# Attention and two feed-forward stages in one kernel: groups of five, four and three slices, two-deep staging

## The chip, the cores and the metric

The kernel runs on one core of a Trainium2 chip. The time is device microseconds of one execution on that core, the median of several runs.

## What is computed

```python
# q, k, v: (2, 8, 768, 64); block 32, window 16
scores_l = where(|i - j| < window, scale * q @ k^T, -1e9)      # local keys
scores_s = scale * q @ (max of k over each block)^T + log(32)  # 24 block keys
a = softmax(concat(scores_l, scores_s))
x = a @ concat(v, mean of v over each block)   # as 1536 tokens x 512
y = ((x @ w_a) * (x @ w_b)) @ w_out            # moe,  inner width 1536
out = leaky(y @ w_in) @ w_out2                 # moe2, inner width 2048, slope 0.01
```

The weights lie in memory as 64-bit floats.

## The kernel before

**Tiles.** The 1536 tokens are three chunks of 512 (`T`, `NC`). A chunk's attention output is four tiles `x` of 128 features, each kept as a high and a low part. The first stage's inner width is 12 slices of 128 (`NF1`), the second's 16. Every product of 32-bit accuracy is three matmuls (high by high, high by low, low by high; `mm3`, L583), so one slice of `x @ w_a` for one chunk is 12 matmuls of 128x512, and the same again for `w_b`.

**Weights.** A piece is one slice of one matrix, 512 KB. `stage` (L300) loads it into a tile `wst` (queue SP, L307 or L310); `convert` turns the 64-bit words into a high and a low part with six steps on DVE (VectorE: L332, L340, L345, L351, L357, L365) and two on ACT (ScalarE: L336, L362). The steps of a piece are spread among the other work of the two engines. `wst` has three buffers, and `convert` asks for up to four pieces ahead. L351 is the last step that reads `wst`. A piece is dropped when its last chunk has used it; 14 homes (`W_EARLY`) hold the converted pieces, 8 more (`W_LATE`) come once attention is over.

**First stage.** The 12 slices go in three groups of `M1` = 4, and for each group all three chunks are done in turn (`units`: group, chunk). Of a unit, each slice gives a product for `w_a` (bank `ps_a`, copied to `g` on ACT, L611), one for `w_b` (bank `ps_b`; DVE multiplies, L615), a high and a low part `gs` (L603 on ACT, L604 on DVE). Then `y_products` multiplies the unit's `gs` by the group's slices of `w_out`, and `gather` (L683, L685, L688) adds the sums of the groups.

**Attention among it.** Chunk 0's attention runs first, with the first two slices of group 0 beside it (`early`, banks a, b, c0, c1). Chunk 1's attention is woven into unit (0, 0), chunk 2's into unit (0, 1): its operations, cut at each large product, wait in `micro`, and `interleave` takes so many of them at each of four points of a slice that they last as long as the unit's remaining slices:

```python
todo = range(len(gs), M1)
...
pace["micro"] = len(micro) / (4 * len(todo) - 1.0)
```

Unit (0, 0) has two slices left to do (`todo`), since two were done beside chunk 0. What attention has per pair of score tiles: scores (L518 on PE, the TensorE; L531 on DVE; L535, the exponential, on ACT), normalizing (L543, L544, L545 on DVE), transposes of the probabilities (L553 on PE), values (L565 on PE, then L576 on DVE writes half of an x tile or a whole). Per half of the heads of a batch, `v` is loaded as `vb` (L154) and its blocks are summed by a set of three adds on POOL (GpSimd, L425) and two reductions on DVE (L435); there are four such sets. Key maxima are DVE's L482, their banks are filled by PE's L472.

**Order.** Each engine runs its instructions in a fixed order, found when the kernel is built: a scheduler with its own costs (L828) takes the operations by priority and by when their inputs and buffers are free. So a change of a number shifts rows on every engine. `q` tiles (L142) have three buffers, the tile `wr` of a conversion two.

Of the kernel before, what the change touches and what calls it, by code (L numbers as in the profile page):

```python
# [12 lines left out]
F32R = mybir.dt.float32r  # L13
I32 = mybir.dt.int32
# [7 lines left out]
def kernel(  # L22
# [14 lines left out]
    P = 128  # L37
# [17 lines left out]
    NF1 = F1 // P  # L55
    NF2 = F2 // P
    T = 512
    NT = B * S
    NC = NT // T
# [3 lines left out]
    assert GT == 2 * P and NB <= KP and KL + KP == P and D == 64 and KT == NP == NE  # L63


    M1 = 4
    M2 = 8
    W_EARLY, W_LATE = 14, 8

    const = ctx.enter_context(tc.tile_pool(name="const", bufs=1))  # L70
    xp = ctx.enter_context(tc.tile_pool(name="xp", bufs=NC * KT))
    wst_p = ctx.enter_context(tc.tile_pool(name="wst", bufs=3))
    wcv_p = ctx.enter_context(tc.tile_pool(name="wcv", bufs=2))
    wsp_p = ctx.enter_context(tc.tile_pool(name="wsp", bufs=W_EARLY))
    acc_p = ctx.enter_context(tc.tile_pool(name="acc", bufs=NE))
    g_p = ctx.enter_context(tc.tile_pool(name="g", bufs=2))
    psum = ctx.enter_context(tc.tile_pool(name="psum", bufs=1, space=bass.MemoryType.PSUM))
    att = ctx.enter_context(ExitStack())
    keep = att.enter_context(tc.tile_pool(name="keep", bufs=1))
    q_p = att.enter_context(tc.tile_pool(name="q", bufs=3))  # L80
    sm_p = att.enter_context(tc.tile_pool(name="sm", bufs=4))
    at_p = att.enter_context(tc.tile_pool(name="at", bufs=2))

# [37 lines left out]
    for j in range(2):  # L121
        t = xp.tile([P, BLK // 2, D], F32, tag="x", name=f"vb{j}")
# [129 lines left out]
    for kind in ("first", "mid", "last"):  # L252
        t = const.tile([P, P], F32, tag=f"negm_{kind}", name=f"negm_{kind}")
# [21 lines left out]

    units = [(s, c) for s in range(NF1 // M1) for c in range(NC)]
    slices2 = [(s * M2 + i, c) for s in range(NF2 // M2) for c in range(NC) for i in range(M2)]
    uses = []  # L280
    for s, c in units:
        fs = range(s * M1, (s + 1) * M1)
        uses += [(nm, f) for f in fs for nm in "ab"] + [("o", f) for f in fs]
    behind = []
    for f, c in slices2:
        uses += [("i", f), *behind]
# [29 lines left out]
    def convert():  # L316

        i = cnt["conv"]
        key = pieces[i]
        while cnt["st"] < min(i + 4, len(pieces)):  # L320
            stage()
        cnt["conv"] += 1
        ww = staged.pop(key).rearrange("p (f two) -> p f two", two=2)
        lo_w, hi_w = ww[:, :, 0], ww[:, :, 1]
        home = "early" if room["early"] else "late"
        assert room[home], key
        room[home] -= 1
        t = {}

        def low():  # L330
            t["r"] = wcv_p.tile([P, 512], I32, tag="wr", name="wr")
            nc.vector.tensor_scalar(  # L332
                out=t["r"], in0=lo_w.bitcast(U32), scalar1=2.0**-29, scalar2=None, op0=ALU.mult
            )
            t["c"] = wcv_p.tile([P, 512], I32, tag="wc", name="wc")
            nc.scalar.activation(out=t["c"].bitcast(F32), in_=hi_w.bitcast(F32), func=AF.Abs)  # L336

        def clamp():
            c = t["c"].bitcast(F32)
            nc.vector.tensor_scalar(  # L340
                out=c, in0=c, scalar1=F_LO, scalar2=F_HI, op0=ALU.max, op1=ALU.min
            )

        def shift():
            nc.vector.tensor_scalar(  # L345
                out=t["c"], in0=t["c"], scalar1=3, scalar2=0x3FFFFFF8,
                op0=ALU.logical_shift_left, op1=ALU.bitwise_and,
            )

        def join():  # L350
            nc.vector.scalar_tensor_tensor(  # L351
                out=t["c"], in0=hi_w, scalar=-0x40000000, in1=t["c"],
                op0=ALU.bitwise_and, op1=ALU.bitwise_or,
            )

        def add():
            nc.vector.tensor_tensor(out=t["c"], in0=t["c"], in1=t["r"], op=ALU.add)  # L357

        def high():
            pool = wsp_p if home == "early" else late["wsp"]  # L360
            t["w"] = pool.tile([P, 2, 512], F32R, tag="wsp", name="wsp")
            nc.scalar.copy(out=t["w"][:, 0], in_=t["c"].bitcast(F32))  # L362

        def rest_of():
            nc.vector.tensor_tensor(  # L365
                out=t["w"][:, 1], in0=t["c"].bitcast(F32), in1=t["w"][:, 0].bitcast(F32),
                op=ALU.subtract,
            )
            w_of[key] = t["w"], home

        bg.extend([low, clamp, shift, join, add, high, rest_of])
# [10 lines left out]
    def step():  # L382
        if bg:
            with tc.issue_after(pace["after"].ins) if pace["after"] is not None else nullcontext():
                bg.pop(0)()
# [3 lines left out]
    def weights(key):  # L389
        i = use_no["at"]  # L390
        assert uses[i] == key, (uses[i], key)
        use_no["at"] += 1
        while key not in w_of:
            if not bg:
                convert()
            step()
        w, home = w_of[key]
        if last_use[key] == i:
            spent.append(home)
            if key[0] != "o":  # L400
                free()
        return w
# [9 lines left out]
    xt = {}  # L412
# [186 lines left out]
        tick(int(cnt["bg"]))  # L599

    def parts(src):
        t = g_p.tile([P, 2, T], F32R, tag="gs", name="gs", bufs=M1)
        nc.scalar.copy(out=t[:, 0], in_=src)  # L603
        nc.vector.tensor_tensor(  # L604
            out=t[:, 1], in0=src, in1=t[:, 0].bitcast(F32), op=ALU.subtract
        )
        return t
# [38 lines left out]
    gs = [b_out(ab0["b", f][1], a_out(ab0["a", f][1])) for f in range(2)]  # L646
# [17 lines left out]
    def first_product(key, src, c):  # L664

        w = weights(key)
        ps = product_bank(key[0])
        for kt in range(KT):
            kt_mm(ps, w, src[c, kt], kt)
            if kt == KT // 2 - 1:  # L670
                interleave()
        return ps
# [3 lines left out]
    def gather(stage, c, e, ps, s, n):  # L676

        if s == 0:
            t = acc_p.tile([P, T], F32, tag="acc", name="acc") if (stage, c) not in late else (
                late[stage, c].tile([P, T], F32, tag="acc", name="acc"))  # L680
            sums[stage, c, e] = t
            if e % 2:
                nc.vector.tensor_copy(out=t, in_=ps)  # L683
            else:
                nc.scalar.copy(out=t, in_=ps)  # L685
            return t
        t = sums[stage, c, e]
        nc.vector.tensor_tensor(out=t, in0=ps, in1=t, op=ALU.add)  # L688
        return t
# [10 lines left out]

    def y_products(s, c, gs):

        ws = [weights(("o", s * M1 + i)) for i in range(M1)]

        def add(ps, e, i):
            mm3(
                ps,
                lambda j: ws[i][:, j, e * P : (e + 1) * P],
                lambda j: gs[i][:, j],
                i == 0, i == M1 - 1,  # L710
            )

        for e in range(0, NE, 2):
            ps = [product_bank("y") for _ in range(2)]

            for i0, i1 in ((0, M1 - 1), (M1 - 1, M1)):
                for j in range(2):
                    for i in range(i0, i1):
                        add(ps[j], e + j, i)
                    if i1 == M1:  # L720
                        if e + j == NE - 1:
                            free()
                        y = gather("y", c, e + j, ps[j], s, NF1 // M1)
                        if s == NF1 // M1 - 1:
                            y_parts(c, e + j, y)
                    interleave()

# [2 lines left out]
            micro.pop(0)[1]()  # L730

    for s, c in units:
        todo = range(len(gs), M1)
        pace["bg"] = {(0, 0): 4, (0, 1): 1, (0, 2): 3}.get((s, c), 1.3)
        if s == 0 and c + 1 < NC:

            last = PER * (sum(len(p) for p in pairs[: c + 2]) - 1) + PV
            micro += [o for o in later_ops if o[0] <= last]
            later_ops = later_ops[len(micro) :]
            pace["micro"] = len(micro) / (4 * len(todo) - 1.0)  # L740
            cnt["credit"] = 0.0
        for i in todo:
            pa = first_product(("a", s * M1 + i), xt, c)
            g = a_out(pa)
            interleave()
            pb = first_product(("b", s * M1 + i), xt, c)
            gs.append(b_out(pb, g))
            interleave()
        drain()
        if (s, c) == (0, NC - 2):  # L750

            att.close()
            late["wsp"] = ctx.enter_context(tc.tile_pool(name="wsp2", bufs=W_LATE))
            acc2 = ctx.enter_context(tc.tile_pool(name="acc2", bufs=2 * NE))
            late.update({(stage, c): acc2 for stage in "yo" for c in range(1, NC)})
            room["late"] = W_LATE
            turn.update({"a": ["a", "t0"], "b": ["b", "t1"], "y": ["c0", "c1", "t2", "t3"]})
            turn["i"] = ["a", "b", "t0", "t1"]
        y_products(s, c, gs)
        gs = []  # L760
# [25 lines left out]
    for f, c in slices2:  # L786
        ps = first_product(("i", f), ysp, c)
# [45 lines left out]
```

## Time and profile before

| | |
|---|---|
| median of 3 runs | 660.8 us (660.76 to 661.89) |
| the profiled execution | 661.53 us, its span 659.8 us |
| PE busy | 96% of the span, 3440 instructions |
| DVE busy | 63%, 952 instructions |
| ACT, POOL busy | 41%, 7% |
| chain that ended last | PE 88%, DVE 6%, POOL 2% |

The span lies between the first and the last instruction; 1.73 us of the profiled execution lie around it. An engine is busy while it has an instruction in work. The chain is followed back from the last instruction to what released each step.

### The profile page before, as it was taken

The numbers are of one execution on the slowest core, as the hardware profiler recorded it, in microseconds if no ns is written. First come the engines' busy times: TensorE is split into PE (matmuls) and PEld (weight loads), VectorE is DVE, ScalarE is ACT, GpSimd is POOL, SyncE is SP. The second block draws the span as 40 slices with busy tenths as digits, with TensorE's granted clock in tenths as the row PEclk, the third lists the DMA queues.
The fourth block names the chain that finished last, engine by engine and source line by source line (L and its number), as shares of the span: only waits on it lengthen the run. The fifth ranks groups of instructions, "written<-read, shape, count | busy, mean of one in ns | idle before, by whom it ended". The sixth has DMA issues, their size and how long they took to land.

```text
span 659.8 us, 9339 instructions
## 1 busy us (share of the span) xinstructions
PE 636.2 (96%) x3440; PEld 519.3 (79%) x3440; DVE 418.1 (63%) x952; ACT 270.8 (41%) x609; POOL 48.5 (7%) x79
## 2 busy tenths in 40 slices
PE   5797989999999999999999999999999999999997
PEld 4576767777888888888888888888888888888886
DVE  3999889955999962699623869732279532422323
ACT  3776787653545421344222535322255322222221
POOL 7254042000000000000000000000000000000000
PEclk9898999999999999999999999999999999999999
DMA  8997744512334430244200232400013000100101
GB/s 196 232 224 194 171 106 108 149 25 65 128 129 138 149 96 1 64 129 127 65 0 1 67 93 73 152 1 0 1 56 105 1 0 1 64 1 1 64 1 64
DMA packets 72622, 53.43 MB, mean 81 GB/s; under 512 B 46208, under 2 KB 66688, under 8 KB 72576
## 3 DMA queue, kind: packets, MB, share of 16 engines
q1 hardware_dynamic: 72576, 52.84, 28.0%
q8 instruction: 27, 0.44, 0.3%
q14 instruction: 19, 0.16, 0.1%
HBM read 49.68 MB, written 3.15 MB: 80 GB/s over the span
## 4 chain that ended last, share of the span: by engine, by line
PE 88%; DVE 6%; POOL 2%; DMA 1%; issue 1%; SPq 1%; ACT 0%; POOLq 0%; DVEq 0%
PE ps_t L583 38%; PE ps_c L583 18%; PE ps_a L583 14%; PE ps_b L583 13%; PE ps_t L518 2%; PE ps_t L565 1%; DVE pm L545 1%; PE ps_t L553 1%; DMA vb<-in_v_dram 1%; DVE pm L531 1%; POOL vb L425 1%; PE ps_t L472 1%; SPq L182 1%; DVE sm L543 0%; DVE acc L688 0%
## 5 line engine op out<-in xcount | busy, mean ns | idle before, releaser
L583 PE MATMUL ps_t<-x,wsp 128*128 128x512 f32 x336 | 78.4, 389 | 0.0
L583 PE MATMUL ps_c<-wsp,gs 128*128 128x512 f32 x288 | 75.9, 389 | 0.0
L583 PE MATMUL ps_t<-wsp,gs 128*128 128x512 f32 x288 | 74.7, 389 | 0.0
L583 PEld LDWEIGHTS ps_t<-x,wsp 128*128 128x128 f32 x336 | 63.1, 188 | 13.1
L583 PE MATMUL ps_t<-ys,wsp 128*128 128x512 f32 x288 | 71.9, 389 | 0.0
L583 PE MATMUL ps_a<-x,wsp 128*128 128x512 f32 x252 | 66.0, 399 | 1.8 <-ACT x L575 1.0
L583 PE MATMUL ps_b<-x,wsp 128*128 128x512 f32 x252 | 65.3, 395 | 0.0
L583 PEld LDWEIGHTS ps_t<-wsp,gs 128*128 128x128 f32 x288 | 54.0, 188 | 11.3
L583 PEld LDWEIGHTS ps_c<-wsp,gs 128*128 128x128 f32 x288 | 54.1, 188 | 11.2
L583 PEld LDWEIGHTS ps_t<-ys,wsp 128*128 128x128 f32 x288 | 54.1, 188 | 11.2
L583 PE MATMUL ps_c<-gs,wsp 128*128 128x512 f32 x240 | 61.0, 394 | 0.0
L336 ACT ACTIVATE wc<-wst 128x512 f32<-128x512 f32 x68 | 45.7, 674 | 28.9 <-DVE wsp L365 28.8
L362 ACT CAST wsp<-wc 128x512 fp32r<-128x512 f32 x68 | 42.1, 622 | 34.4 <-DVE wc L357 27.5
L583 PEld LDWEIGHTS ps_a<-x,wsp 128*128 128x128 f32 x252 | 46.8, 190 | 11.9 <-ACT x L575 1.3
L790 DVE SCALAR_TENSOR_TENSOR h<-h,ps_t 128x512 f32<-128x512 f32 x24 | 16.5, 686 | 60.3 <-ACT h L789 60.3
L583 PEld LDWEIGHTS ps_b<-x,wsp 128*128 128x128 f32 x252 | 46.6, 189 | 9.5 <-issue 0.3
L365 DVE TENSOR_TENSOR wsp<-wc,wsp 128x512 fp32r<-128x512 f32 x68 | 46.9, 693 | 8.5 <-ACT wsp L362 8.5
L583 PEld LDWEIGHTS ps_c<-gs,wsp 128*128 128x128 f32 x240 | 44.4, 188 | 9.6 <-DVE wr L332 0.2
L357 DVE CUSTOM_DVE_ANT_0 wc<-wc,wr 128x1024 uint16<-128x1024 uint16 x68 | 48.8, 718 | 0.5
L604 DVE TENSOR_TENSOR gs<-h,gs 128x512 fp32r<-128x512 f32 x48 | 33.1, 690 | 22.8 <-ACT gs L603 22.7
L583 PE MATMUL ps_t<-gs,wsp 128*128 128x512 f32 x192 | 47.5, 389 | 0.0
L351 DVE SCALAR_TENSOR_TENSOR wc<-wst,wc 128x512 int32<-128x512 int32 x68 | 46.6, 688 | 0.3
(94 smaller groups left out, 863.5 us busy)
## 6 DMA issues: line engine op xcount, KB each, us to landing
wst<-in_moe_w_out_dram SPq DMA_DIRECT2D x28, 512.0 KB, 3.3
wst<-in_moe_w_in_dram SPq DMA_DIRECT2D x16, 512.0 KB, 3.7
wst<-in_moe_w_a_dram SPq DMA_DIRECT2D x12, 512.0 KB, 4.4
wst<-in_moe_w_b_dram SPq DMA_DIRECT2D x12, 512.0 KB, 3.7
k<-in_k_dram SPq DMA_DIRECT2D x16, 192.0 KB, 3.6
vb<-in_v_dram SPq DMA_DIRECT2D x8, 384.0 KB, 5.4
out_dram<-acc SPq DMA_DIRECT2D x12, 256.0 KB, 2.0
q<-in_q_dram SPq DMA_DIRECT2D x16, 128.0 KB, 2.9
```

The costliest lines, as they stand in the source:

```text
L182: nc.sync.dma_start(out=t[p0 : p0 + o1 - o0, c, w0:w1, :], in_=src)
L336: nc.scalar.activation(out=t["c"].bitcast(F32), in_=hi_w.bitcast(F32), func=AF.Abs)
L351: nc.vector.scalar_tensor_tensor(out=t["c"], in0=hi_w, scalar=-0x40000000, in1=t["c"], op0=ALU.bitwise_and, op1=ALU.bitwise_or,)
L357: nc.vector.tensor_tensor(out=t["c"], in0=t["c"], in1=t["r"], op=ALU.add)
L362: nc.scalar.copy(out=t["w"][:, 0], in_=t["c"].bitcast(F32))
L365: nc.vector.tensor_tensor(out=t["w"][:, 1], in0=t["c"].bitcast(F32), in1=t["w"][:, 0].bitcast(F32), op=ALU.subtract,)
L425: nc.gpsimd.tensor_tensor(out=a, in0=a, in1=b, op=ALU.add)
L472: nc.tensor.transpose(ps[:, i * P : (i + 1) * P], k2[:, g * (GT // P) + i].rearrange("p c d -> p (c d)"), ident)
L518: nc.tensor.matmul(out=ps[h, w, :], lhsT=qt[h, w * W : (w + 1) * W], rhs=kts[h, (g * G + w) * SC : (g * G + w) * SC + P], start=True, stop ...
L583: nc.tensor.matmul(out=ps, lhsT=w(a), rhs=x(b), start=first and j == 0, stop=last and j == 2)
L604: nc.vector.tensor_tensor(out=t[:, 1], in0=src, in1=t[:, 0].bitcast(F32), op=ALU.subtract)
L790: nc.vector.scalar_tensor_tensor(out=h, in0=h, scalar=0.01, in1=ps, op0=ALU.mult, op1=ALU.max)
```

## The change

The first stage's slices go in groups of five, four and three (`group1`), and whatever depended on four slices takes the group's own range. One more home for converted weights (15) and one more `gs` buffer (5) hold the wider group. Staged weights `wst` and queries `q` are two deep instead of three, and `wr` is one deep. The products, conversions, loads and gathers are the same in number: only `todo` of unit (0, 0) has now three slices, that of unit (0, 1) five. In the changed kernel line numbers are higher by 1 to 3 (L583 is L585, L576 is L578, L351 is L353).

```diff
-    M1 = 4
+
+    M1 = (5, 4, 3)
     M2 = 8
-    W_EARLY, W_LATE = 14, 8
+    W_EARLY, W_LATE = 15, 8
...
-    wst_p = ctx.enter_context(tc.tile_pool(name="wst", bufs=3))
+    wst_p = ctx.enter_context(tc.tile_pool(name="wst", bufs=2))
...
-    q_p = att.enter_context(tc.tile_pool(name="q", bufs=3))
+    q_p = att.enter_context(tc.tile_pool(name="q", bufs=2))
...
-    units = [(s, c) for s in range(NF1 // M1) for c in range(NC)]
+    assert sum(M1) == NF1
+    group1 = [range(sum(M1[:s]), sum(M1[: s + 1])) for s in range(len(M1))]
+    units = [(s, c) for s in range(len(M1)) for c in range(NC)]
...
-        fs = range(s * M1, (s + 1) * M1)
-        uses += [(nm, f) for f in fs for nm in "ab"] + [("o", f) for f in fs]
+        uses += [(nm, f) for f in group1[s] for nm in "ab"] + [("o", f) for f in group1[s]]
...
-            t["r"] = wcv_p.tile([P, 512], I32, tag="wr", name="wr")
+            t["r"] = wcv_p.tile([P, 512], I32, tag="wr", name="wr", bufs=1)
...
-        t = g_p.tile([P, 2, T], F32R, tag="gs", name="gs", bufs=M1)
+        t = g_p.tile([P, 2, T], F32R, tag="gs", name="gs", bufs=max(M1))
...
-        todo = range(len(gs), M1)
+        todo = group1[s][len(gs) :]
...
-        for i in todo:
-            pa = first_product(("a", s * M1 + i), xt, c)
+        for f in todo:
+            pa = first_product(("a", f), xt, c)
             g = a_out(pa)
             interleave()
-            pb = first_product(("b", s * M1 + i), xt, c)
+            pb = first_product(("b", f), xt, c)
```

`y_products` takes `n = len(ws)` slices instead of `M1`, and `len(M1)` groups.

What moves, at two places. The first is on PE, where it comes to its first product on chunk 1's attention output (`x_0_1110` before, `x_0_1141` now). The rows ahead of it before:

```order
L553 MATMUL ps_t_1295<-ident,pm 128x128 x4
L518 MATMUL ps_t_1373<-kts_94,qt 64x128 x8
L553 MATMUL ps_t_1366<-ident,pm 128x128 x4
L565 MATMUL ps_t_1393<-pt,vw_99 64x64 x8
L500 MATMUL ps_t_1339<-ident,q 128x128 x4
L565 MATMUL ps_t_1393<-pt,vw_99 64x64 x8
L452 MATMUL ps_t_1417<-v_1223,ident 24x64 x4
L518 MATMUL ps_t_1443<-kts_91,qt 64x128 x8
L553 MATMUL ps_t_1424<-ident,pm 128x128 x4
L583 MATMUL ps_a<-x_0_1110,wsp 128x512 x3
L583 MATMUL ps_b<-x_0_524,wsp 128x512 x2
L583 MATMUL ps_a<-x_1_1113,wsp 128x512
```

and now:

```order
L520 MATMUL ps_t_1421<-kts_94,qt 64x128 x8
L454 MATMUL ps_t_1465<-v_1257,ident 24x64 x4
L567 MATMUL ps_t_1441<-pt,vw_99 64x64 x16
L520 MATMUL ps_t_1491<-kts_91,qt 64x128 x8
L585 MATMUL ps_a<-x_0_524,wsp 128x512 x3
L585 MATMUL ps_a<-x_1_668,wsp 128x512 x3
L585 MATMUL ps_a<-x_2_786,wsp 128x512 x3
L585 MATMUL ps_a<-x_3_917,wsp 128x512 x3
L555 MATMUL ps_t_1484<-ident,pm 128x128 x4
L502 MATMUL ps_t_1522<-ident,q 128x128 x4
L585 MATMUL ps_b<-x_0_524,wsp 128x512 x2
L585 MATMUL ps_a<-x_0_1141,wsp 128x512 x3
```

Four more rows of products on chunk 0 (`ps_a<-x_0_524` to `x_3_917`, 12 matmuls of a slice's `w_a`) stand ahead of it here, and another 12 (a slice's `w_b`) some rows above the first one shown; scores, transposes and values are the same ones in nearly the same order.

The second is on DVE, where it writes the second half of that output, which the PE rows above wait for (`x_0_1110<-ps_t_1393` before):

```order
L543 TENSOR_SCALAR sm<-sm 128x4
L345 TENSOR_SCALAR wc<-wc 128x512
L544 RECIPROCAL sm<-sm 128x4
L351 SCALAR_TENSOR_TENSOR wc<-wst,wc 128x512
L545 TENSOR_TENSOR pm<-pm,sm 128x512
L357 ISA wc<-wc,wr 128x1024
L543 TENSOR_SCALAR sm<-sm 128x4
L576 TENSOR_TENSOR x_0_1110<-ps_t_1393,x_0_1110 128x256
L544 RECIPROCAL sm<-sm 128x4
L545 TENSOR_TENSOR pm<-pm,sm 128x512
L365 TENSOR_TENSOR wsp<-wc,wsp 128x512
L576 TENSOR_TENSOR x_1_1113<-ps_t_1393,x_1_1113 128x256
```

and now (`x_1_1144<-ps_t_1441`, second half of the same tiles):

```order
L342 TENSOR_SCALAR wc<-wc 128x512
L334 TENSOR_SCALAR wr<-wst 128x512
L545 TENSOR_SCALAR sm<-sm 128x4
L347 TENSOR_SCALAR wc<-wc 128x512
L367 TENSOR_TENSOR wsp<-wc,wsp 128x512
L546 RECIPROCAL sm<-sm 128x4
L353 SCALAR_TENSOR_TENSOR wc<-wst,wc 128x512
L547 TENSOR_TENSOR pm<-pm,sm 128x512
L578 TENSOR_TENSOR x_0_1141<-ps_t_1441,x_0_1141 128x256
L359 ISA wc<-wc,wr 128x1024
L545 TENSOR_SCALAR sm<-sm 128x4
L578 TENSOR_TENSOR x_1_1144<-ps_t_1441,x_1_1144 128x256
```

The normalizing steps and the x tiles are the same; the conversion steps among them (`wc`, `wr`, `wsp`) belong to other pieces, and two more whole conversions stand ahead of this place than before.

## Rows read from the trace of the kernel before

**Rows 1.** The page, part 1: busy us, share of the span and instructions of each engine.

```profile
PE 636.2 (96%) x3440; PEld 519.3 (79%) x3440; DVE 418.1 (63%) x952; ACT 270.8 (41%) x609; POOL 48.5 (7%) x79
```

**Rows 2.** Stretches: bounds and length in us, then busy us (instructions) of each engine.

```profile
86.00:99.00 13.00, 10.10 (x134) 7.81 (x132) 12.86 (x47) 9.90 (x38) 4.12 (x6) 1.00 0.46 119
99.00:166.00 67.00, 67.00 (x513) 51.89 (x514) 49.96 (x157) 38.03 (x110) 6.26 (x3) 1.00 0.30 85
166.00:655.00 489.00, 489.00 (x2159) 404.90 (x2158) 284.56 (x518) 166.76 (x277) 0.00 (x0) 1.00 0.18 58
```

**Rows 3.** Timeline of PE around 97 us: start us, length us, instruction, [wait <- releaser].

```profile
97.12 0.73 PE L583 MATMUL ps_a<-x,wsp 128*128 128x512 f32 x2 [0.74 <-DVE x L576]
```

**Rows 4.** The chain that ended last, two pieces: start us, length us, what.

```profile
96.74 0.33 DVE x L576
...
177.40 2.72 PE ps_a L583 x12
```

**Rows 5.** Timeline of DVE, two stretches: where one step follows at once on another.

```profile
28.63 0.16 DVE L543 TENSOR_SCALAR sm<-sm 128x4 f32<-128x4 f32 x1
...
29.30 0.69 DVE L357 CUSTOM_DVE_ANT_0 wc<-wc,wr 128x1024 uint16<-128x1024 uint16 x1
29.91 0.68 DVE L576 TENSOR_TENSOR x<-ps_t,x 128x512 fp32r<-128x512 f32 x1
...
69.51 0.42 DVE L332 TENSOR_SCALAR wr<-wst 128x512 int32<-128x512 uint32 x1
69.85 0.42 DVE L340 TENSOR_SCALAR wc<-wc 128x512 f32<-128x512 f32 x1
70.18 0.69 DVE L604 TENSOR_TENSOR gs<-g,gs 128x512 fp32r<-128x512 f32 x1
70.78 0.43 DVE L345 TENSOR_SCALAR wc<-wc 128x512 int32<-128x512 int32 x1
```

**Rows 6.** Timeline of DVE, 64 to 97 us: three of its five waits.

```profile
66.43 0.69 DVE L615 TENSOR_TENSOR g<-ps_b,g 128x512 f32<-128x512 f32 x1 [0.86 <-ACT g L611]
...
83.44 0.29 DVE L531 CUSTOM_DVE_ANT_0 pm<-ps_t,negm_first 128x128 f32<-128x128 f32 x1 [1.98 <-PE ps_t L553]
...
85.47 0.29 DVE L531 CUSTOM_DVE_ANT_0 pm<-ps_t,negm_first 128x128 f32<-128x128 f32 x1 [1.09 <-PE ps_t L518]
```

**Rows 7.** Timeline of POOL, 53 to 87 us: the third and fourth set of v adds.

```profile
53.49 3.12 POOL L425 TENSOR_TENSOR vb<-vb,vb 96x512 f32<-96x512 f32 x2 [5.51 <-DMA q<-in_q_dram]
...
57.78 1.59 POOL L425 TENSOR_TENSOR vb<-vb 96x512 f32<-96x512 f32 x1
...
81.92 2.51 POOL L425 TENSOR_TENSOR vb<-vb,vb 96x512 f32<-96x512 f32 x2 [3.91 <-DMA vb<-in_v_dram]
...
84.76 1.27 POOL L425 TENSOR_TENSOR vb<-vb 96x512 f32<-96x512 f32 x1
```

**Rows 8.** Timeline of DVE, steps beside a set of adds: first, second, third set.

```profile
15.13 1.61 DVE L545 TENSOR_TENSOR pm<-pm,sm 128x512 f32<-128x512 f32 x1
...
34.32 1.64 DVE L357 CUSTOM_DVE_ANT_0 wc<-wc,wr 128x1024 uint16<-128x1024 uint16 x1
...
53.73 1.76 DVE L545 TENSOR_TENSOR pm<-pm,sm 128x512 f32<-128x512 f32 x1
55.41 1.23 DVE L543 TENSOR_SCALAR sm<-sm 128x4 f32<-128x4 f32 x1
...
58.17 1.75 DVE L545 TENSOR_TENSOR pm<-pm,sm 128x512 f32<-128x512 f32 x1
59.85 0.68 DVE L482 TENSOR_REDUCE ks<-ps_t 128x16 f32<-128x512 f32 x1
```

**Rows 9.** Timeline of PE around 60 us.

```profile
60.58 0.69 PE L472 MATMUL ps_t<-ident,k 128*128 128x128 f32 x2 [3.91 <-DVE ks L482]
```

**Rows 10.** The page, part 6: loads, KB each, median us from issue to landing.

```profile
wst<-in_moe_w_a_dram SPq DMA_DIRECT2D x12, 512.0 KB, 4.4
...
vb<-in_v_dram SPq DMA_DIRECT2D x8, 384.0 KB, 5.4
```

More of the change, by code (lines that the diff above doesn't have):

```diff
@@ L701, in y_products @@
     def y_products(s, c, gs):
-        ws = [weights(("o", s * M1 + i)) for i in range(M1)]
+        ws = [weights(("o", f)) for f in group1[s]]
+        n = len(ws)
         def add(ps, e, i):
@@ L709, in add @@
                 lambda j: gs[i][:, j],
-                i == 0, i == M1 - 1,
+                i == 0, i == n - 1,
             )
@@ L714, in y_products @@
             ps = [product_bank("y") for _ in range(2)]
-            for i0, i1 in ((0, M1 - 1), (M1 - 1, M1)):
+            for i0, i1 in ((0, n - 1), (n - 1, n)):
                 for j in range(2):
@@ L719, in y_products @@
                         add(ps[j], e + j, i)
-                    if i1 == M1:
+                    if i1 == n:
                         if e + j == NE - 1:
                             free()
-                        y = gather("y", c, e + j, ps[j], s, NF1 // M1)
-                        if s == NF1 // M1 - 1:
+                        y = gather("y", c, e + j, ps[j], s, len(M1))
+                        if s == len(M1) - 1:
                             y_parts(c, e + j, y)
```

## The prediction

> **What bounds the kernel now.** The page first: PE is busy 636.2 of 659.8 us [rows 1], so at most some 24 us are to be had from waits, and the change takes no product away. Then the busy times by stretch: from 99 us on PE is busy for the whole of every stretch, 67.00 of 67 and 489.00 of 489, and DVE has time over, 49.96 and 284.56 [rows 2]. From 86 to 99 us it is the other way round: DVE 12.86 of 13.00, PE 10.10 [rows 2]. So the run has two halves, and a change is worth what it moves at the seam. The timeline of PE shows the seam: the last wait of PE ends at 97.12 us, released by DVE's L576, the second half of chunk 1's first x tile [rows 3], and the chain has that step directly ahead of PE's products [rows 4]. After it PE runs without a pause to the end. The end time is therefore: when DVE finishes that half tile, plus the PE work not done by then. DVE steps taken or added before it count in full; PE work moved ahead of it comes off; and what DVE does behind it is covered, as long as DVE stays ahead.
>
> **What the change moves past the seam.** Unit (0, 0) has three slices left instead of two, with the same attention of chunk 1 spread among them. I counted, in both orders, the rows up to the seam: DVE up to the half tile that PE waits for, PE up to the row that waits. In the new order the tightest pair is one tile further on: DVE's second half of chunk 1's second x tile, the last DVE row shown, and PE's transposes of q (L502, the last PE row shown but two), which want the bank that this half tile empties.
> - DVE has every attention step as often as before, and beyond that two more conversions, one more product for `g` (L615), one more `gs` part (L604) and one more half x tile (L576). On a busy DVE the price of a step is from one start to the next: L357 0.61 us, L332 and L340 0.34 and 0.33, L604 0.60 [rows 5], a half x tile 0.33 [rows 4]. L351 and L365, as large as L357, I take at 0.60, L345 as L340, L615 as L604. A conversion is 3 x 0.33 + 3 x 0.60 = 2.8 us. So 2 x 2.8 + 0.60 + 0.60 + 0.33 = **+7.1 us**.
> - PE has 108 large products ahead of the seam in place of 85. Twelve take 2.72 us [rows 4], one 0.227: 23 x 0.227 = **-5.2 us**, work that no longer stands behind. Net so far +1.9.
> - DVE's waits for PE. Between chunk 0's last x tile and the seam DVE stands still five times, 4.75 us in all; the first and the two longest are 0.86, 1.98 and 1.09 [rows 6]. They come from PE running late behind DVE: adding step prices along both orders, PE's largest lateness before these is 7.55 us, and the nearest DVE step that wants PE leaves it 3.42; the difference 4.1 and some 0.6 for signals make the 4.75. In the new order PE's lateness there is at most 6.2 us and the two nearest DVE steps leave 5.9 and 6.2, because DVE has conversions in between: 0.3 + 0.6 = 0.9 us is left. So 0.9 - 4.75 = **-3.85 us**; bounds 0 (all of them stay) and -4.75.
> - POOL's v adds. When a set meets a busy DVE, DVE's steps stretch. Third set, 3.12 + 1.59 = 4.71 us [rows 7]: L545 goes from 53.73 to 55.41 and from 58.17 to 59.85, 1.68 each in place of 0.60, and L543 takes 1.23 in place of 0.16 [rows 8, 5], together 3.2 us lost. The first and second set cost about 0.9 and 1.0, by L545 of 1.61 and L357 of 1.64 [rows 8], as steps of this size take 0.69 undisturbed [rows 5]. The fourth, 2.51 + 1.27 = 3.78 us [rows 7], fell into the two waits of 1.98 and 1.09 [rows 6] and cost some 0.3. With those waits gone it meets work. Bounds for the third and fourth together: at the first set's 0.9 each, 1.8 in place of 3.5, -1.7; both at full length, 8.5, +5.0. If the third stays as it is and the fourth pays the mean of the other three, 1.7, it is +1.4; if both pay that mean, 0. I take the middle, **+0.7**, since which steps of DVE a set meets is new for both.
>
> Sum: 7.1 - 5.2 - 3.85 + 0.7 = **-1.25 us**. From the profiled execution, 661.53, that is 660.3; it stands 0.7 above the median of 660.8, so against the median 659.55, **659.5 us**.
>
> The rule that speaks against this is that of the Trainium skill, "SBUF — State Buffer", "Who interferes with whom": VectorE and GpSimd share a pair of ports, a vector instruction with two inputs in SBUF contends with a GpSimd one that reads SBUF, and whoever holds the pair in a two-port mode makes the other block for its whole instruction. That L545, with two inputs in SBUF, was stretched to 1.68 agrees with it; that the third set cost 3.2 of its 4.71 us shows the block was not complete here. By a full block of the fourth set the sum would be +1.5 instead of -1.25 (third rival).
>
> **What I cost at nothing.**
> - Everything after the seam: groups of four and three, gathers of other shapes, the second stage. PE is never out of work from 99 us on and DVE is free for 17 of the next 67 us and 204 of the 489 behind [rows 2]. Directly after the seam, where chunk 2's attention is spread over five slices instead of four, PE's later needs leave DVE 2.5 to 3.4 us by the step prices; that cover is gone if DVE loses that much there again.
> - `wst` two deep. From a piece's last reading step (L351) to the first use of the piece two on, DVE has at least 5.8 us of steps in the new order; a piece lands in 4.4 us at the median [rows 10]. If the queue holds a load back by over 1.4 us, DVE waits. `q` and `wr` two and one deep: the DVE order has the two readers further apart still.
> - The PE stall of 3.91 us at 60.58 [rows 9]. It stands behind a key maximum that in DVE's row has conversions ahead of it. In the new order, 3.1 us of these stand behind chunk 0's last x tile instead; the stall shrinks, but DVE does them before the seam all the same. Likewise SP has two instead of three staged pieces ahead of the second v load, which lands (5.4 us, [rows 10]) the earlier. Both are given back at the seam, so neither is in the sum.
>
> **The rivals.**
> 1. *Larger gain.* The third set meets steps no dearer than the first two sets did (1.0 in place of 3.2), and the fourth again falls into what waits DVE has left. For: the first two cost so little [rows 8], and the v load is earlier. Against: DVE is fuller there than before. 1.9 - 3.85 - 2.2 = -4.15 us: 656.6 us. Chance 0.20.
> 2. *Slower, the waits stay.* The 24 products now stand in PE's row ahead of transposes and scores that DVE's L531 wants, and each dozen puts these off by 2.72 us. If PE gets to them later than the counted 5.9 us of cover, DVE waits as much as before, and the seam pays for the added conversions. For: the two longest waits now are just of this kind, L531 behind L553 and L518 [rows 6]. Against: DVE's added conversions stand in the same gaps. 1.9 + 0.7 = +2.6: 663.4 us. It decides for slower once more than 2.2 us of the 4.75 stay (1.9 - 2.55 + 0.7 is about 0), and for more than 0.2% once 3.5 stay. Chance 0.18.
> 3. *The fourth set pays in full.* POOL holds DVE up for all of the 3.78 us, 3.5 more than now, and the third set is as before: 1.9 - 3.85 + 3.5 = +1.55: 662.3 us. For: L545 at 1.68 [rows 8]. Against: the first two sets. Chance 0.12, half of it within 0.2%.
> 4. *The change does nothing at the seam.* The gap is only handed on: DVE's waits shrink by just the 1.9 + 0.7 = 2.6 us that it has more to do, and 2.1 stay: 660.8 us. For: in the old order too PE's lateness set the waits. Against: the counted cover of 5.9 us. Chance 0.08.
>
> **How the numbers follow.** 0.2%, 1.3 us, is about what a measurement of this kernel can tell from no change. My forecast, chance 0.42, has its own range from 658.0 (all waits gone, ports +0) to 661.1 (1.5 us of waits left, ports +1.4): 1.9 - 4.75 = -2.85 and 1.9 - 3.25 + 1.4 = +0.05, with 0.3 for the prices of steps on the upper side. Half of it lies beyond 0.2% faster, half within. Faster: 0.21 + 0.20 = 0.41. Same: 0.21 + 0.06 + 0.08 = 0.35. Slower: 0.18 + 0.06 = 0.24. The range takes in half of the larger gain and all but the worse half of the second rival: 656.4 to 663.6 us, and leaves out about 0.2.
>
> **What would show it.** In the profile after: PE's last wait should again end on a half x tile of chunk 1, at about 101 us (97.1, 5.2 for the products done earlier, less 1.25), and PE should be full from there. The busy time of PE ahead of it should be 5 us larger. DVE's five waits between chunk 0's last x tile and there should come to about 1 us instead of 4.75. The fourth set of adds should stretch L545 or a conversion step to over 1 us. DVE should wait nowhere for a `wst` load before 100 us beyond what it does now. I am wrong if PE waits again behind the seam, if DVE's waits for L518 or L553 still come to over 3 us, or if the stretch of DVE beside the adds is far from 4 us for sets three and four.

## The result, and the profile after

The changed kernel takes 667.37 us at the median of 4 runs (666.36 to 669.0), the kernel before 661.35 beside it: a ratio of 1.0092, 95% interval 1.007 to 1.0113. It is slower by about 6 us. The forecast was 659.5, with a range up to 663.6.

The profiled execution took 667.19 us, its span is 665.4. The page's busy times, which answer to [rows 1]:

```profile
PE 639.8 (96%) x3440; PEld 520.2 (78%) x3440; DVE 418.4 (63%) x952; ACT 269.5 (41%) x609; POOL 46.6 (7%) x79
```

The instructions of each engine are the same in number; PE is busy 3.6 us longer. Where the time went shows in the stretches of 5 us after 85 us (bounds, length, busy us of PE, PEld, DVE, ACT and POOL with their instructions, granted clock, DMA share, GB/s). The changed kernel:

```profile
85.00:90.00 5.00, 3.01 (x54) 2.19 (x50) 1.35 (x10) 3.15 (x15) 3.20 (x3) 1.00 0.78 213
90.00:95.00 5.00, 2.66 (x6) 2.16 (x7) 4.42 (x11) 1.04 (x2) 2.70 (x3) 0.53 0.02 3
95.00:100.00 5.00, 5.00 (x43) 4.00 (x43) 3.64 (x14) 2.43 (x7) 0.00 (x0) 0.79 0.60 173
```

From 85 to 90 us DVE, which was to be the full engine here, has work for 1.35 of 5 us, and behind that PE stands, and then runs at a granted clock of 0.53. The kernel before had a clock of 1.00 there and DVE at 12.86 of 13 us [rows 2]. The timelines name the wait. DVE first (start us, length us, instruction, [wait <- releaser]):

```profile
90.58 1.07 DVE L437 TENSOR_REDUCE v<-vb 96x32 f32<-96x256 f32 x2 [4.02 <-POOL vb L427]
91.57 0.72 DVE L367 TENSOR_TENSOR wsp<-wc,wsp 128x512 fp32r<-128x512 f32 x1
```

The two reductions of the fourth set of v sums wait 4.02 us for POOL's adds, and behind them in DVE's fixed order stands L367, the last conversion step of a piece. PE wants that piece:

```profile
87.31 0.73 PE L585 MATMUL ps_b<-x,wsp 128*128 128x512 f32 x2
92.34 4.64 PE L585 MATMUL ps_b<-x,wsp 128*128 128x512 f32 x10 [4.30 <-DVE wsp L367]
...
103.72 2.57 PE L585 MATMUL ps_a<-x,wsp 128*128 128x512 f32 x10 [0.98 <-DVE wsp L367]
```

PE waits 4.30 us, and the ten products after it take 4.64 us where ten take 2.57 at 103.72. DVE then waits for these slow products in its turn:

```profile
97.02 0.69 DVE L617 TENSOR_TENSOR g<-ps_b,g 128x512 f32<-128x512 f32 x1 [1.31 <-PE ps_b L585]
```

PE's last wait ends at 103.72, not at 97.12 [rows 3], and on a converted piece (L367), not on a half x tile. Why the adds were late is in the chain of waits, around 82 us (start us, length us, what):

```profile
81.84 0.42 SPq L183
82.26 0.05 issue
82.31 0.03 SPq L155
82.34 0.03 issue
82.37 4.21 DMA vb<-in_v_dram
86.58 0.02 issue
86.61 0.02 POOLq L427
86.62 0.09 issue
86.72 2.49 POOL vb L427 x2
```

The chain comes from SP, which issues window loads (L183) one after another, then half of the fourth v load (L155), which lands in 4.21 us; then come the adds, the reductions, the conversion step and PE. SP's own timeline, changed kernel:

```profile
74.80 7.46 SPq L183 DMA_DIRECT2D vw<-in_v_dram  x12
82.37 0.36 SPq L155 DMA_DIRECT2D vb<-in_v_dram  x1
```

and the kernel before:

```profile
75.38 0.33 SPq L154 DMA_DIRECT2D vb<-in_v_dram  x1
76.01 8.66 SPq L182 DMA_DIRECT2D vw<-in_v_dram  x12
```

Twelve window loads, 0.62 us of SP's time each, have changed places with one v load. It goes out 7.0 us later, although its buffer was free earlier than before (the third set's reductions begin at 72.46 us, before at 74.19). The other half of the same v load went out much earlier, at 58.72 us instead of 72.43; but the adds take both halves.

### The profile page after: what moved, and what is told of

It is laid out like the page before. It is cut to its first block, busy times and chain, and to the rows that moved or that the text cites. A ratio compares the mean times of both kernels' runs of the same rounds, so it can differ in the third digit from the quotient of the medians.

```text
span 665.4 us, 9361 instructions
## 1 busy us (share of the span) xinstructions
PE 639.8 (96%) x3440; PEld 520.2 (78%) x3440; DVE 418.4 (63%) x952; ACT 269.5 (41%) x609; POOL 46.6 (7%) x79
## 4 chain that ended last, share of the span: by engine, by line
PE 88%; DVE 5%; POOL 2%; issue 1%; DMA 1%; ACT 1%; SPq 1%; POOLq 0%; DVEq 0%; ACTq 0%
PE ps_t L585 36%; PE ps_c L585 18%; PE ps_b L585 14%; PE ps_a L585 14%; PE ps_t L520 3%; PE ps_t L567 1%; PE ps_t L555 1%; DVE pm L533 1%; SPq L183 1%; DVE wsp L367 1%; DVE pm L547 1%; DMA vb<-in_v_dram 1%; ACT pm L537 1%; DVE sm L545 1%; POOL vb L427 1%
## 5 line engine op out<-in xcount | busy, mean ns | idle before, releaser
L585 PE MATMUL ps_c<-wsp,gs 128*128 128x512 f32 x288 | 75.6, 389 | 0.0
L585 PE MATMUL ps_t<-wsp,gs 128*128 128x512 f32 x288 | 74.4, 389 | 0.0
L585 PE MATMUL ps_b<-x,wsp 128*128 128x512 f32 x264 | 70.1, 405 | 4.3 <-DVE wsp L367 4.3
L585 PE MATMUL ps_t<-x,wsp 128*128 128x512 f32 x312 | 73.0, 389 | 0.0
L585 PE MATMUL ps_a<-x,wsp 128*128 128x512 f32 x264 | 69.2, 399 | 3.1 <-DVE x L578 1.3
L585 PE MATMUL ps_t<-ys,wsp 128*128 128x512 f32 x288 | 71.9, 389 | 0.0
L338 ACT ACTIVATE wc<-wst 128x512 f32<-128x512 f32 x68 | 45.8, 674 | 62.0 <-DVE wsp L367 18.4
L585 PEld LDWEIGHTS ps_t<-x,wsp 128*128 128x128 f32 x312 | 58.6, 188 | 12.1
L585 PEld LDWEIGHTS ps_t<-wsp,gs 128*128 128x128 f32 x288 | 54.1, 188 | 11.2
L585 PEld LDWEIGHTS ps_c<-wsp,gs 128*128 128x128 f32 x288 | 54.1, 188 | 11.2
L585 PEld LDWEIGHTS ps_t<-ys,wsp 128*128 128x128 f32 x288 | 54.1, 188 | 11.2
L585 PEld LDWEIGHTS ps_b<-x,wsp 128*128 128x128 f32 x264 | 50.0, 193 | 15.8 <-DVE wsp L367 4.7
L585 PE MATMUL ps_c<-gs,wsp 128*128 128x512 f32 x246 | 62.2, 392 | 0.0
L585 PEld LDWEIGHTS ps_a<-x,wsp 128*128 128x128 f32 x264 | 48.3, 188 | 15.0 <-DVE x L578 1.7
L585 PEld LDWEIGHTS ps_c<-gs,wsp 128*128 128x128 f32 x246 | 45.7, 188 | 9.8 <-issue 0.3
L367 DVE TENSOR_TENSOR wsp<-wc,wsp 128x512 fp32r<-128x512 f32 x68 | 49.4, 728 | 5.5 <-ACT wsp L364 5.5
L353 DVE SCALAR_TENSOR_TENSOR wc<-wst,wc 128x512 int32<-128x512 int32 x68 | 47.2, 694 | 0.2
L359 DVE CUSTOM_DVE_ANT_0 wc<-wc,wr 128x1024 uint16<-128x1024 uint16 x68 | 46.6, 685 | 0.7
L585 PE MATMUL ps_t<-gs,wsp 128*128 128x512 f32 x186 | 46.2, 390 | 0.0
```

Of the source, the lines that this page charges most:

```text
L353: nc.vector.scalar_tensor_tensor(out=t["c"], in0=hi_w, scalar=-0x40000000, in1=t["c"], op0=ALU.bitwise_and, op1=ALU.bitwise_or,)
L367: nc.vector.tensor_tensor(out=t["w"][:, 1], in0=t["c"].bitcast(F32), in1=t["w"][:, 0].bitcast(F32), op=ALU.subtract,)
L585: nc.tensor.matmul(out=ps, lhsT=w(a), rhs=x(b), start=first and j == 0, stop=last and j == 2)
```

## The experiments

Theory A: the late half of one v load, met early in DVE's order, costs the 6 us. Rival B: two-deep staging, or the conversions added ahead of the seam, cost it, and the v wait only covers that.

**One load moved.** In the changed kernel the last v load is asked for a little earlier in the list of attention operations:

```diff
-                        add(-4, LOAD, load_vb, b, vi)
+                        add(-8 if (b, vi) == (1, 1) else -4, LOAD, load_vb, b, vi)
```

PE's and ACT's rows stay as they are. With the load, the two reductions move up by two rows on DVE in the trace, and on POOL, against what was expected, the adds move ahead of two copies of key maxima (L491).

> The changed kernel, with one load asked for earlier: the second half of the fourth v load (L155) stands on SP ahead of nine of the twelve window loads (L183) that it stood behind; apart from it one pair of reductions (L437) moves up by three rows on DVE, and every other engine keeps its row order. Theory A (the late v load): it is issued at about 77 us instead of 82.4, the adds end about 5 us sooner, DVE's wait of 4.02 us at 90.58 falls below 0.5, PE's wait of 4.30 at 92.34 is gone, and the ten products behind it run at 0.23 us each instead of 0.46, 2.3 us more; the time falls from 667.2 to 660 to 662 us. Rival B (the added conversions ahead of the seam and the two-deep staging cost the time, and the v wait only covers it): other waits take its place, the time stays over 665 us.

Measured: 0.9992 of the kernel before, interval 0.9973 to 1.0011. It ran again for its trace:

> The same kernel as the first of the earlier four (the second half of the fourth v load ahead of nine window loads), for its trace. Theory A: L155 is issued at about 77 us, the last set of adds runs from about 81 to 85 us, DVE waits under 0.5 us for them, PE has no wait of over 1 us between 85 and 100 us, and the granted clock stays at 1.00 there; 660 to 663 us.

Measured: 1.0001 (0.9981 to 1.0021). And a third time, beside the changed kernel:

> The changed kernel with the second half of the fourth v load moved ahead of nine window loads, beside the changed kernel on the same chip: theory A expects 5.5 to 7 us less than it, within 0.2% of the kernel before.

> The changed kernel itself, beside the version with the v load moved on the same chip: theory A expects 0.8 to 1.1% over the kernel before, and DVE's wait of about 4 us for the adds again.

Measured: 1.0000 (0.9987 to 1.0012) with the load moved, 1.0091 (1.0074 to 1.0107) for the changed kernel, 662.38 against 668.91 us. In that second trace of the changed kernel DVE waited for the adds only 1.34 us, less than expected, because it came later to them, after 2.15 us for PE; PE's wait for L367 was 2.91 us. The adds set the start of the reductions all the same (91.69 us). The chain of waits leads from DVE's 2.15 us back to a staged piece (a weight loaded into `wst`) that was late for ACT's L338, the first step to read it; PE waited for that piece and then ran slowly:

```profile
75.26 0.67 ACT L338 ACTIVATE wc<-wst 128x512 f32<-128x512 f32 x1 [2.75 <-DMA wst<-in_moe_w_b_dram]
```

```profile
78.02 0.73 PE L585 MATMUL ps_a<-x,wsp 128*128 128x512 f32 x2 [1.70 <-ACT wsp L364]
...
78.91 4.15 PE L585 MATMUL ps_a<-x,wsp 128*128 128x512 f32 x10
```

With the load moved (the run for its trace, span 658.5 us) SP, PE and DVE show:

```profile
75.36 0.54 SPq L155 DMA_DIRECT2D vb<-in_v_dram  x1
75.99 5.16 SPq L183 DMA_DIRECT2D vw<-in_v_dram  x9
```

```profile
87.67 2.56 PE L585 MATMUL ps_b<-x,wsp 128*128 128x512 f32 x10 [0.53 <-DVE wsp L367]
...
99.84 0.63 PE L502 MATMUL ps_t<-ident,q 128*128 128x128 f32 x4 [0.55 <-PE ps_t L555]
```

```profile
85.50 1.11 DVE L437 TENSOR_REDUCE v<-vb 96x32 f32<-96x256 f32 x2 [0.26 <-POOL vb L427]
```

The wait of 4.02 us is 0.26, that of 4.30 is 0.53, the ten products take 2.56. Row for row with the changed kernel, the ten products begin at 87.67 instead of 92.34. Theory A holds, rival B falls as the cause of the 6 us: groups, staging and added conversions are all still there, and the loss is gone. Of the 6.9 us between these two traces, 0.9 are there before the reductions (the same half tile, L578, at 81.66 us and at 80.77; at 81.70 in the third run's trace, whose span is 659.4 us), 3.8 are the wait for the adds (4.02 and 0.26), 1.3 are DVE's wait for the slow products, and the rest comes later on DVE.

**Is it DVE's order, or the sums?** The v load stays late; the two reductions are held behind an x tile, ten rows further down, by an issue-order edge (NoSync: no wait for the tile), so that DVE goes on with L367 (shortened):

```diff
+            for o in last_sums:
+                tc.add_manual_dep(o().ins, x_done[5].ins.name, NoSync)
```

> The changed kernel, the v load as late as it is there, but the last set's two reductions on DVE (L437) are held behind the x tile that stands nine rows further down, so that the conversion step L367 and what follows it go ahead of them. If the wait counts because DVE's fixed order holds up a weight that PE wants (theory A), DVE works through most of the 4 us, PE's wait of 4.30 us shrinks to under 1.5, and the time is 660.5 to 663 us. If it counts because the sums themselves are late (their placing on PE, L454, and what follows), PE waits there instead, and the time stays over 665 us.

Measured: 1.0046 (1.0027 to 1.0065), 665.21 us: half of the loss is back, more time than expected. PE's big wait did go (0.42 us are left of it), but the adds now meet a DVE with work, and its steps stretch:

```profile
86.87 0.60 DVE L342 TENSOR_SCALAR wc<-wc 128x512 f32<-128x512 f32 x1
87.39 1.23 DVE L556 TENSOR_SCALAR sm<-sm 128x4 f32<-128x4 f32 x1
88.54 0.68 DVE L367 TENSOR_TENSOR wsp<-wc,wsp 128x512 fp32r<-128x512 f32 x1
89.14 1.51 DVE L347 TENSOR_SCALAR wc<-wc 128x512 int32<-128x512 int32 x1
90.57 0.17 DVE L557 RECIPROCAL sm<-sm 128x4 f32<-128x4 f32 x1
```

L342 takes 0.52 to the next start instead of 0.33, L556 (the same step as L543) 1.15 instead of some 0.1, L347 1.43 instead of 0.33: 2.3 us of the 4.02 saved are lost again beside POOL's adds, which ran from 85.91 to 90.37. So DVE's fixed order cost about half. The other half, some 3 us, stays as long as the adds are late; the rows show 2.3 of it as stretched steps, and the rest wasn't followed.

**A late load in the kernel before.** There the load was held behind the same twelve window loads by an issue-order edge (shortened):

```diff
+            if (b, i, j) == (1, 1, 0):
+                tc.add_manual_dep(ld.ins, vw_last[max(vw_last)].ins.name, NoSync)
```

> The kernel before, three deep and in groups of four, with the second half of the fourth v load held behind the twelve window loads it stood ahead of; the order then has both reductions about ten rows ahead of the seam. Theory A: the load is issued at about 84 us instead of 75.4, the adds end at about 92, DVE wants them at about 92.5; less than 1.5 us slower than before. If a late v load costs by itself, whatever DVE's order: slower by 3 to 6 us.

Measured: 1.0033 (1.0012 to 1.0054), some 2.2 us, over the 1.5 expected: PE waited 1.06 us for the reductions and 1.59 for an x tile. So a late load costs about a third of the 6 us even with the reductions near the seam.

**The buffers alone.**

```diff
-    wst_p = ctx.enter_context(tc.tile_pool(name="wst", bufs=3))
+    wst_p = ctx.enter_context(tc.tile_pool(name="wst", bufs=2))
...
-    q_p = att.enter_context(tc.tile_pool(name="q", bufs=3))
+    q_p = att.enter_context(tc.tile_pool(name="q", bufs=2))
...
-            t["r"] = wcv_p.tile([P, 512], I32, tag="wr", name="wr")
+            t["r"] = wcv_p.tile([P, 512], I32, tag="wr", name="wr", bufs=1)
```

> The kernel before with groups of four, and of the change only the buffers: wst and q two deep, wr one deep. Its SP order, too, has the second half of the fourth v load behind twelve window loads, but its DVE order has the two reductions seven rows ahead of the seam, not forty. Theory A: DVE meets them when the adds are nearly done, the wait is under 1.5 us, and the time is within 1.5 us of the kernel before. Rival B (two-deep staging makes conversions wait for loads): slower than before by 3 to 6 us, with DVE waiting for wst loads.

Measured: 1.0015 (0.9997 to 1.0032). Already here the v load stands behind the twelve window loads, so it is the buffers that moved it; with groups of four the reductions stand seven rows ahead of the seam, and little is lost. The same with the load moved up in the same way:

> Groups of four with the buffers two deep, as in the earlier run of that name, and the second half of the fourth v load ahead of eight of the twelve window loads. In that earlier run PE waited 2.12 us for the window sums and 1.19 us for the v sums between 90 and 97 us and the time was 0.15% above the kernel before. Theory A: both waits go, the time falls by 1 to 3 us, to 0.1 to 0.4% below the kernel before: the first version here that would be faster than it. Rival: the waits for the sums stood beside DVE work that bounds the seam anyway, and the time stays within 0.1% of the earlier run's.

Measured: 1.0012 (0.9999 to 1.0024), no gain: the rival was right here. Its trace no longer has PE's waits for the sums, but one of 1.39 us for L545 and one of 1.87 for L332, at 78.22, after ACT's L336 had waited 2.57 us for a staged piece at 75.62.

**What does the lost clock cost?** The changed kernel, late load and all, with the first product of the waiting slice done 16 times over (shortened):

```diff
+        if (key, c) == (("b", 3), 0) and src is xt:
+            for _ in range(16):
+                nc.tensor.matmul(out=ps, lhsT=w[:, 0, 0:P], rhs=src[c, 0][:, 0], start=True, stop=True)
```

> The changed kernel, v load as late as there, with 16 products more: the first product of the slice at which PE waits 4.30 us is done 16 times over with the same operands, which leaves the result as it is and keeps PE at work for 3.6 us of the wait. If the fall of the granted clock to half behind the wait costs what its rows say (ten products at 0.46 us in place of 0.23, 2.1 to 2.3 us), the clock stays at 1.00 and the time falls from 667.2 to 664.5 to 665.5 us although PE does 3.6 us more. If the lost clock is hidden by DVE, which PE waits for once more at 103.7 us, the time stays within 0.7 us of 667.2.

Measured: 1.0079 (1.0062 to 1.0097), 667.44 us. Its stretch and PE's waits:

```profile
90.00:95.00 5.00, 3.89 (x18) 2.89 (x17) 3.37 (x8) 1.04 (x2) 3.68 (x4) 1.00 0.05 12
```

```profile
93.40 2.56 PE L585 MATMUL ps_b<-x,wsp 128*128 128x512 f32 x10 [1.11 <-DVE wsp L367]
...
103.24 2.55 PE L585 MATMUL ps_a<-x,wsp 128*128 128x512 f32 x10 [0.76 <-DVE wsp L367]
```

The clock stays at 1.00 and the ten products take 2.56 us, 2.1 less. DVE's wait of 1.31 us for them is gone too. From the start of the reductions to the end of the last wait for L367 this trace takes 11.60 us, the changed kernel 13.14:

```profile
91.64 1.10 DVE L437 TENSOR_REDUCE v<-vb 96x32 f32<-96x256 f32 x2 [4.48 <-POOL vb L427]
...
96.69 0.67 DVE L617 TENSOR_TENSOR g<-ps_b,g 128x512 f32<-128x512 f32 x1
```

So the half clock was not wholly hidden by DVE; between these two traces it is worth some 1.5 us. The time doesn't show it: in this trace the adds ended 1.05 us later (91.60 instead of 90.55), so that the last wait ends only 0.5 us earlier, and 1.0079 against 1.0092 and 1.0091 is 0.8 us, less than the intervals can tell from nothing or from 1.5. Of the 3.6 us that PE is longer busy in the changed kernel, 2.1 are these ten products.

**All v loads by preference**, in both kernels:

```diff
+            with tc.high_priority():
-            nc.sync.dma_start(
+                nc.sync.dma_start(
```

> The changed kernel with all four v loads asked for with preference, so that each goes out on SP as soon as its buffer is free; the last one then stands ahead of all twelve window loads. Rows on all engines shift somewhat. Theory A: no wait for the adds, as fast as with the one load moved, 659.5 to 662 us. Rival: the reshuffled order finds another wait; over 663 us.

> The kernel before with the same preference for all four v loads. There the last v load already goes out when its buffer is free, so theory A expects no gain: within 1.3 us of the kernel before.

Measured: 1.0007 (0.9993 to 1.002) for the changed kernel, 1.0022 (1.0011 to 1.0034) for the kernel before. The first loses nothing that can be measured, as expected; the second is 1.5 us slower, a little more than the 1.3 allowed for, with rows moved on all engines; its cause wasn't followed up. No version was faster than the kernel before. The groups of five, four and three with three-deep staging weren't tried, nor was it tried which of the three buffers moved the load.

## Why the prediction was wrong

**What failed: a queue that was read at one place only.** Of SP's v loads the prediction says only that "two instead of three staged pieces" stand ahead of the second, which lands the earlier, and that this is given back at the seam: nothing in the sum. It did not follow SP to the fourth v load, whose second half had moved from ahead of twelve window loads to behind them; nor did it ask where on DVE the reductions stood that wait for it. In DVE's order they are now 41 rows ahead of the half tile that was to be the seam (`x_1_1144`); of the two before, the second stood 19 rows ahead of the half tile there (`x_0_1110`). Both were in the orders. The price was written nowhere: 7.0 us later on SP, 4.02 of wait on DVE, 6.9 us of the profiled time (667.19 against 660.29 with the load moved).

**The fourth set of adds**, "meets work" in the prediction, +0.7 in the sum. In the changed kernel it met a DVE that stood waiting for it. With the load moved it did meet work and cost less than the 1.7 us of the mean: the dearest step beside it was this one, 0.6 us over its due, since much of what DVE did then were L533 steps, which took 0.21 each as ever:

```profile
82.59 1.18 DVE L359 CUSTOM_DVE_ANT_0 wc<-wc,wr 128x1024 uint16<-128x1024 uint16 x1
83.80 0.53 DVE L334 TENSOR_SCALAR wr<-wst 128x512 int32<-128x512 uint32 x1
84.31 0.29 DVE L533 CUSTOM_DVE_ANT_0 pm<-ps_t,negm_first 128x128 f32<-128x128 f32 x1
```

That is some 0.8 us for the fourth set. The third set, too, met cheaper steps than before, some 1.9 us in place of 3.2 (1.43 and 1.69 to the next start, in place of 0.60 each):

```profile
51.04 1.51 DVE L547 TENSOR_TENSOR pm<-pm,sm 128x512 f32<-128x512 f32 x1
52.47 1.76 DVE L367 TENSOR_TENSOR wsp<-wc,wsp 128x512 fp32r<-128x512 f32 x1
54.16 0.16 DVE L545 TENSOR_SCALAR sm<-sm 128x4 f32<-128x4 f32 x1
```

So with the load moved both sets together cost some 2.7 us in place of 3.5, -0.8 where the sum has +0.7.

**`wst` two deep, put at nothing.** The prediction looked at DVE's steps, and of these none waited directly for a load. But ACT's L338 reads a piece first, and it did wait. The kernel before, where no step waited for a staged piece between 45 and 80 us, then the changed kernel:

```profile
64.36 0.68 ACT L336 ACTIVATE wc<-wst 128x512 f32<-128x512 f32 x1
```

```profile
65.40 0.67 ACT L338 ACTIVATE wc<-wst 128x512 f32<-128x512 f32 x1 [0.98 <-DMA wst<-in_moe_w_a_dram]
...
74.34 0.67 ACT L338 ACTIVATE wc<-wst 128x512 f32<-128x512 f32 x1 [1.50 <-DMA wst<-in_moe_w_b_dram]
```

In the second trace these two waits are 2.44 and 2.75 us, and DVE's L342 waits 0.89 and 0.83 behind them; with the load moved they are 0.26 and 0.54, and with the reductions held back there are none, so they vary between traces. What they cost the time wasn't measured apart. They are not the 6 us, since those went with the v load.

**What held.** DVE's waits for PE: 4.75 us were to shrink to 0.9. Ahead of the reductions, L533's three waits in the changed kernel come to 0.50 + 0.57 + 0.57 = 1.64 (one of 0.54 for ACT comes on top), with the load moved two come to 0.54 + 0.55 = 1.09. In the second trace of the changed kernel, behind the late piece, they come to 2.15 + 0.57 = 2.72. The seam: with the load moved PE's last wait ended at 99.84 us in one trace and at 100.69 in another, with 101 forecast, in the first just behind DVE's half tile (L578, 99.33 to 99.74), though the profile puts that wait down to PE. The stall of 3.91 us [rows 9] is gone; the largest wait of PE between 45 and 70 us is one of 1.25, at 62.15.

**The sum without the v wait** was -1.25 us. With the load moved, three comparisons give 0.9992, 1.0001 and 1.0000, the tightest 0.9987 to 1.0012, or 0.9 us less to 0.8 more: no gain that can be measured. By that interval the sum was too good by 0.4 to 2 us. Besides the adds, which were put too dear, a term put too good shows in the stretch from PE's last wait to the end of the span, before and with the load moved (two traces):

```profile
97.12:659.80 562.68, 559.03 (x2683) 458.85 (x2683) 338.25 (x680) 206.12 (x388) 6.26 (x3) 1.00 0.20 63
```

```profile
99.84:658.50 558.66, 555.07 (x2660) 454.78 (x2660) 331.75 (x664) 201.60 (x382) 4.04 (x4) 1.00 0.20 62
100.69:659.40 558.71, 555.03 (x2660) 454.98 (x2660) 331.69 (x664) 201.71 (x382) 4.04 (x4) 1.00 0.19 62
```

PE has 23 matmuls fewer behind the seam (2660 for 2683), as counted, but needs only 4.0 us less, not 5.2; where the 1.2 us went wasn't followed. The seam itself moved by 2.7 and 3.6 us, with 7.1 - 3.85 + 0.7 = 3.95 forecast.

**The rivals.** The slower one that was priced, waits of DVE for PE that stay, is not what happened: with the load moved they shrank and the loss was gone. The one that did happen was not on the list. That the fourth set pays in full did not happen either.

## What to carry to other kernels

Where a scheduler sets every queue, a change of buffer counts moves loads: follow each queue through the whole stretch that bounds the end, and for each load that has changed places, find the instruction that waits for its data and what stands behind that on its engine. A wait in a fixed order costs by what it holds up, not by its own data: the v sums were wanted late, the weight behind them at once. When a wait is moved out of the way, ask what its work collides with then: over half of the wait saved went to DVE steps stretched beside POOL. And when a buffer gets fewer, look at the first reader of its data on every engine, not only on the one that is full.

## What had not been expected of the hardware

After the wait of 4.30 us the granted clock fell to about half (0.53 from 90 to 95 us) and ten products took 4.64 us instead of 2.56, the lower of the two levels of 1.2 and 2.4 GHz; with PE kept at work through most of the wait (idle for 1.11 us) it stayed at 1.00. What this cost the time stays open: the slow products took 2.1 us more, DVE waited 1.31 us for them, and the measured times differ by 0.8 us, within their intervals. A small step can also be stretched as much as a large one beside POOL's adds: L556, four columns, took 1.15 us to the next start instead of some 0.1, L347, 512 columns, 1.43 instead of 0.33.
